# Polysketch attention followed by a squared-ReLU FFN: the sketch features of k in four column tiles of the array, and S loaded repeated over the partitions

## The chip, the cores and the metric

The kernel runs on one core of a Trainium2 chip. The metric is device time in microseconds (us) of one execution; 187.35 us is the median of three runs before the change. A profile of one execution is at hand, with the start and duration of every instruction.

The engines are named as the profile names them: PE is the matrix engine (PEld its weight loads), DVE the vector engine, ACT the scalar engine, POOL the GpSimd engine, SP the engine that issues most of the DMAs.

## The reference, cut to what matters

```python
q, k, v: (4, 4, 1088, 32)   # batch, heads, tokens, head_dim; float32
S1, S2:  (8, 32)
def phi(x):                                   # 64 features per token
    a = einsum('rd,bhsd->bhsr', S1, x)
    b = einsum('rd,bhsd->bhsr', S2, x)
    return einsum('bhsi,bhsj->bhsij', a, b).reshape(..., 64)
q_p, k_p = phi(q), phi(k)
kv  = einsum('bhsf,bhsd->bhfd', k_p, v)       # 64 x 32 per head
z   = k_p.sum(over tokens)
att = (q_p @ kv) / (q_p . z + 1e-6)
x   = att as (4352 tokens, 128)
out = relu(x @ w_in)**2 @ w_out               # w_in (128, 2048), w_out (2048, 128)
```

## The kernel before, in words

**Two stages.** A prologue of some 14 us, written out by hand, computes the sums kv and z of batch 0 and the first 256 columns of xT, the transposed attention output. After it comes the long part: the FFN goes over the 4352 token columns in ten chunks (256, 384, 448, ... wide), each in units of one or two blocks of 128 hidden channels: first matmul (line 589, tile pg), relu on ACT (line 598), square on ACT or DVE (lines 606 and 608), second matmul (line 627, tile po). The attention of the remaining columns and of batches 1 to 3 is woven in between. The order of this part comes from a planner (class `_Order`), which works with fixed costs per operation and due times; the order of each engine's instructions is thus settled when the kernel is built. The diff doesn't touch the planner's entries.

**The prologue, in the order of PE's queue.** (1) Ten matmuls on constants (`keep_warm(W0)`, line 678). (2) `a_kf` (line 311): for the nine 128-token tiles of k, one matmul each (line 314) with the 128 transposed token columns as weights (`kt0`, 128 x 128) and `sf` (128 x 64) as the moving operand. `sf` holds S1 and S2 transposed, once for each of four heads in that head's 32 rows, and zero elsewhere. A float32 matmul appears in the profile as two weight loads and two matmuls, so there are 18 records of each. (3) `q0` (line 729): the sketch of the first 256 query columns, with `sq` as the weights. (4) `a_kv0` (line 390): 36 matmuls that sum the key features times v (tile kvp). (5) The denominator (lines 754 and 794), the products with z (line 801, with `s2f` and `zm`), the spreading of kv (line 433, with `irep`), the numerator (line 794), one warm matmul, the sketch `qc` of the next query columns (line 304), one more warm matmul, and then the FFN's first unit.

**The other engines in the prologue.** DVE transposes k (line 291, tile kt) and S (line 688, tile s_T); it multiplies the key features (`a_kp0`, line 330, four instructions); transposes q (line 297); it makes `bd` and `zm` from kvp (lines 764 and 775), copies kvp (line 773, tile kvt), and makes the reciprocal of the denominator and the first 256 columns of xT (lines 814 to 819). ACT copies half of each kf tile to SBUF (line 320, tile kb). POOL writes constants, copies S into several layouts (lines 693 to 716), converts the four quarters of w_in (line 671) as they land, and fills `sfk` (lines 786 and 789), the weights for the k sketch of later batches.

**S before.** S1 and S2 are loaded once each into 8 rows of a 32 x 32 tile `s_nat` (lines 217 and 218, on ACT's queue, after DVE's memset of line 216). DVE transposes it to `s_T` (32 x 32). From there the layouts are made by copies: four into `sf` (line 693, one per head, on POOL, DVE and ACT), five into `sq` (lines 696 to 703), four more into `sf[:, 64:96]` (line 708), from which `sw` is copied (line 716), and `s2f` is transposed by DVE (line 747).

**Loads.** SP issues, in this order, k (two pieces), q (256 columns), v, the rest of v, q, w_in and w_out. Eight completion counters are used in rotation, and a load waits at issue for the load eight before it to have landed.

## Time and profile before

| what | value |
|---|---|
| median of three runs (187.19 to 187.91) | 187.35 us |
| span of the profiled execution | 186.17 us |
| median less that span, taken as what lies around it (the profiled execution has no time of its own besides the span) | 1.18 us |
| PE busy | 180.4 us, 97% of the span |
| ACT busy | 147.1 us, 79% |
| DVE busy | 108.6 us, 58% |
| POOL busy | 36.5 us, 20% |
| first FFN matmul (line 589) in the timeline | 14.04 us |
| PE busy between 20 and 180 us | 160.00 us of 160.00 |

A line of the timeline gives the start in us, the busy time in us, the engine, the line of the kernel, the operation, the tile written and the tiles read, the shapes, and in brackets the idle time before it and what ended it. Times of single instructions are taken from the records behind that view. The view of one line of the kernel gives minimum, median and maximum of their duration in ns. A line of the chain that ended last gives start, length, and what worked.

### The profile page before, as it was taken

To read this page: it belongs to the slowest core of one execution; us is meant where nothing else is said; L and a number is where in the kernel's file an instruction comes from. 1 tells how busy PE (TensorE), PEld (TensorE's weight loads), DVE (VectorE), ACT (ScalarE), POOL (GpSimd) and SP (SyncE) were. 2 spreads that over 40 slices of the span, in tenths; PEclk is the share of its full clock that TensorE was granted. 3 is DMA by queue.
4 is the path that set the end of the run, shared out by engine and by line. 5 is a ranking of instruction groups with operands and counts; after the bars stand their busy time and mean duration, and the time that the engine had idled before them with its cause. 6 is when DMAs were issued, how large, how long until landed. Compare 5 with 4: busy or idle time off the path is not lost.

```text
span 186.2 us, 3768 instructions
## 1 busy us (share of the span) xinstructions
PE 180.4 (97%) x1417; PEld 105.2 (56%) x1418; DVE 108.6 (58%) x242; ACT 147.1 (79%) x281; POOL 36.5 (20%) x162
## 2 busy tenths in 40 slices
PE   8998999999999999999999999999999999999991
PEld 2766766656555566454554545554545554555791
DVE  4979979969982599599324972997122113112210
ACT  3518769868978887797899897897999999988960
POOL 2745405328300000860000003820000000000000
PEclk9999999999999999999999999999999999999999
DMA  5799800100049500001871200002103000300211
GB/s 185 192 297 310 192 4 5 28 4 0 0 55 267 130 2 4 4 0 24 200 186 19 42 0 4 0 0 38 22 0 58 0 0 0 56 0 0 32 28 28
DMA packets 24673, 11.25 MB, mean 60 GB/s; under 512 B 18000, under 2 KB 23120, under 8 KB 24656
## 3 DMA queue, kind: packets, MB, share of 16 engines
q1 hardware_dynamic: 24144, 10.82, 25.0%
q10 hardware_dynamic: 512, 0.20, 0.4%
q8 instruction: 11, 0.18, 0.4%
q14 instruction: 6, 0.05, 0.1%
HBM read 8.78 MB, written 2.23 MB: 59 GB/s over the span
## 4 chain that ended last, share of the span: by engine, by line
PE 90%; DMA 4%; SPq 1%; POOL 1%; issue 1%; DVE 0%; ACT 0%; ACTq 0%
PE po L627 60%; PE pg L589 18%; PE nd L542 3%; DMA w_in<-in_moe_w_in_dram 3%; PE kvp L408 2%; PE pol L622 2%; PE po L622 2%; PE qc L304 2%; DMA s_nat<-in_S_dram 2%; PE kc L344 1%; SPq L194 1%; POOL sfk L789 0%; ACT gt L598 0%; POOL w_in L671 0%; SPq L203 0%
## 5 line engine op out<-in xcount | busy, mean ns | idle before, releaser
L627 PE MATMUL po<-g,w_o 128*128 128x512 f32 (+3 forms) x288 | 133.0, 546 | 0.3 <-PE pg L589 0.3
L589 PE MATMUL pg<-xT,w_in 128*128 128x512 f32 (+3 forms) x160 | 104.8, 665 | 0.6 <-ACT gt L598 0.5
L598 ACT ACTIVATE gt<-pg 128x512 f32<-128x512 f32 (+3 forms) x145 | 80.7, 561 | 21.7 <-PE pg L589 21.2
L606 ACT ACTIVATE g<-gt 128x512 f32<-128x512 f32 (+2 forms) x122 | 71.8, 603 | 2.7
L627 PEld LDWEIGHTS po<-g,w_o 128*128 128x128 f32 x288 | 53.0, 189 | 30.0 <-issue 19.8
L589 PEld LDWEIGHTS pg<-xT,w_in 128*128 128x128 f32 x160 | 30.1, 189 | 31.7 <-issue 14.3
L608 DVE TENSOR_TENSOR g<-gt 128x512 f32<-128x512 f32 (+3 forms) x23 | 15.1, 660 | 45.9 <-ACT gt L598 45.9
L449 POOL COPY kv<-kvt 32x64 f32<-32x64 f32 x48 | 11.7, 243 | 65.4 <-DVE kvt L426 63.3
L503 POOL COPY rd<-rc 32x9 f32<-32x9 f32 (+2 forms) x80 | 16.7, 209 | 13.1 <-DVE rc L495 9.8
L512 DVE STREAM_SHUFFLE qa<-qc 128x576 f32<-128x576 f32 (+2 forms) x20 | 11.6, 652 | 0.0
L527 DVE TENSOR_TENSOR qp<-qa,qb 128x576 f32<-128x576 f32 (+2 forms) x20 | 10.8, 603 | 0.0
L475 DVE STREAM_TRANSPOSE qt<-qc 128x576 f32<-128x576 f32 (+2 forms) x10 | 5.8, 615 | 5.8 <-PE qc L304 5.8
L631 DVE STREAM_TRANSPOSE oT<-po 128x512 f32<-128x512 f32 (+3 forms) x9 | 5.9, 655 | 5.0 <-PE po L627 5.0
L361 DVE TENSOR_TENSOR kp<-fs 128x576 f32<-128x576 f32 x12 | 8.4, 752 | 0.1
L542 PE MATMUL nd<-qp,kv 32*32 32x288 f32 (+2 forms) x320 | 6.8, 353 | 0.0
L559 DVE TENSOR_TENSOR xT<-nd,bc 128x576 fp32r<-128x576 f32 (+2 forms) x10 | 5.6, 600 | 0.9 <-PE nd L542 0.7
L512 DVE STREAM_SHUFFLE qb<-qc 128x576 f32<-128x576 f32 (+2 forms) x10 | 6.0, 648 | 0.0
L542 PEld LDWEIGHTS nd<-qp,kv 32*32 32x32 f32 x320 | 3.8, 103 | 3.8 <-issue 2.2
L297 DVE STREAM_TRANSPOSE qT<-qn 128x192 f32<-128x192 f32 (+3 forms) x11 | 5.9, 566 | 0.0
L552 DVE STREAM_TRANSPOSE bc<-rd 128x576 f32<-128x576 f32 (+2 forms) x10 | 5.8, 602 | 0.2
L622 PE MATMUL pol<-w_o,g 128*128 128x128 f32 x32 | 5.7, 275 | 0.0
L622 PE MATMUL po<-w_o,g 128*128 128x128 f32 x32 | 5.7, 274 | 0.0
(96 smaller groups left out, 92.3 us busy)
## 6 DMA issues: line engine op xcount, KB each, us to landing
kn<-in_k_dram SPq DMA_DIRECT2D x3, 544.0 KB, 5.4
qn<-in_q_dram SPq DMA_DIRECT2D x3, 544.0 KB, 6.9
vn<-in_v_dram SPq DMA_DIRECT2D x9, 144.0 KB, 5.5
w_in<-in_moe_w_in_dram SPq DMA_DIRECT2D x4, 256.0 KB, 5.2
w_o<-in_moe_w_out_dram SPq DMA_DIRECT2D x4, 256.0 KB, 7.1
out_dram<-oT SPq DMA_DIRECT2D x12, 64.0 KB, 2.0
out_dram<-oT SPq DMA_DIRECT2D x8, 56.0 KB, 1.9
out_dram<-oT SPq DMA_DIRECT2D x8, 48.0 KB, 1.8
```

What stands on the lines that cost most here:

```text
L361: nc.vector.tensor_tensor(out=_ap(st[b, "kp"], 0, 128, 64 * NT * h, [[64, NT], [8, 8], [1, 8]]), in0=_ap(fs, 0, 128, o, [[32, NT], [1, 8], ...
L449: nc.gpsimd.tensor_copy(_ap(st[b, "kv"], 32 * c, 32, 64 * h, [[32, E], [1, 32]]), _ap(st["kvt"], 32 * h, 32, 0, [[64, E], [1, 32]]),)
L503: nc.gpsimd.tensor_copy(st[b, "rd", i0][32 * h : 32 * h + 32, n * c : n * c + n], st["rc"][32 * c : 32 * c + 32, n * h : n * h + n],)
L512: nc.vector.stream_shuffle(in_=banks(st[b, "qc", i0], 2 * x, 0, m), out=_ap(st[b, which, i0], 0, 128, 2 * m * x, [[m, 2], [1, m]]), mask=m ...
L527: nc.vector.tensor_tensor(out=st[b, "qp", i0, e][:, r], in0=st[b, f"qa{e}", i0][:, r], in1=st[b, "qb", i0][:, r], op=mult,)
L542: nc.tensor.matmul(nd[32 * h : 32 * h + 32, 512 * c : 512 * c + m], kv[r, o : o + 32], qp[r, m * h : m * h + m], start=(e == 0), stop=(e = ...
L589: nc.tensor.matmul(st["pg", u][:, n * i : n * i + n], w_in[:, 128 * (d0 + i) : 128 * (d0 + i) + 128], xT[:, c0 : c0 + n],)
L598: nc.scalar.activation(gt[:, 0:w], st["pg", u][:, 0:w], Relu)
L606: nc.scalar.activation(g2[:, 0:w], gt[:, 0:w], Square)
L608: nc.vector.tensor_tensor(out=g2[:, 0:w], in0=gt[:, 0:w], in1=gt[:, 0:w], op=mult)
L622: nc.tensor.matmul(po[x // 128][:, 0:128], g[:, x : x + 128], w, start=(d == 0), stop=(d == NB - 1),)
L627: nc.tensor.matmul(po[0][:, 0:n], w, g, start=(d == 0), stop=(d == NB - 1))
```

## The change

S1 and S2 are each loaded by one DMA that repeats their 8 rows 16 times over the 128 partitions (128 runs of 128 bytes), into the two halves of `s_nat` (128 x 64). S1 is the first DMA of ACT's queue, and S2 is put on SP between the two pieces of k. No memset stands ahead of them. One DVE transpose (128 x 64) then gives S transposed in all partitions.

The copies become products with masks: `own_h` (which 32 rows a partition is in) and `own_q` (even or odd block of 32), made by DVE from the identity matrix. `sf` is one product on POOL; `sq` is two ACT copies with a per-partition scale and one product on POOL; `sw` is a small memset and a copy each; `sfk` is one product on POOL, ahead of the w_in conversions instead of behind them. `s2f` is gone: `s_nat[:, 32:64]` takes its place.

`a_kf` issues four matmuls per 128-token tile, each with 32 columns of weights, into 32 partitions of the output. There are nine warm matmuls in place of ten. Two memsets go from DVE to POOL, the copy of kvp goes from DVE to ACT, `bd`'s second half is made before `zm`, and two transposes of q (`a_qT` at 8 and 14) move from ahead of the `bd` products to behind `zm`.

```diff
-    W0, W3, W4 = 10, 1, 1
+    W0, W3, W4 = 9, 1, 1
...
-    nc.vector.memset(s_nat[:], 0.0)
-    nc.scalar.dma_start(s_nat[0:8, :], S1[:, :])
-    nc.scalar.dma_start(s_nat[8:16, :], S2[:, :])
+    def load_s(eng, x, src):
+        eng.dma_start(
+            s_nat[:, 32 * x : 32 * x + 32],
+            bass.AP(src.tensor, src.offset, [[0, 16], [D, 8], [1, D]]),
+        )
+
+    load_s(nc.scalar, 0, S1)
     load_k(nc.sync, 0, 0, 512)
+    load_s(nc.sync, 1, S2)
     load_k(nc.sync, 0, 512, S)
...
+    nc.vector.tensor_reduce(
+        out=own_h[:, :], in_=_ap(iden, 0, 128, 0, [[32, 4], [1, 32]]), op=add, axis=AX
+    )
+    nc.vector.tensor_tensor(out=own_q[:, :], in0=own_h[:, 0:2], in1=own_h[:, 2:4], op=add)
...
-    nc.vector.memset(kT[:, S:SP], 0.0)
-    nc.vector.memset(qT[:, S:SP], 0.0)
...
-            nc.tensor.matmul(
-                _ap(kf, 0, 128, 32 * t, [[32 * n, 2], [1, 32]]),
-                kt0[:, 128 * (t0 + t) : 128 * (t0 + t) + 128],
-                sf[:, 0:64],
-            )
+            for c in range(4):
+                o = 128 * (t0 + t) + 32 * c
+                nc.tensor.matmul(
+                    _ap(kf, 32 * c, 32, 32 * t, [[32 * n, 2], [1, 32]]),
+                    kt0[:, o : o + 32],
+                    sf[:, :],
+                )
...
+    nc.gpsimd.tensor_tensor(
+        out=_ap(sf, 0, 128, 0, [[32, 2], [8, 4], [1, 8]]),
+        in0=_ap(s_T, 0, 128, 0, [[32, 2], [8, 4], [1, 8]]),
+        in1=_ap(own_h, 0, 128, 0, [[0, 2], [1, 4], [0, 8]]),
+        op=mult,
     )
+    for x in range(2):
+        nc.scalar.activation(
+            _ap(sq, 0, 128, 64 * x, [[8, 8], [1, 8]]), _ap(s_T, 0, 128, 32, [[0, 8], [1, 8]]),
+            Copy, scale=own_q[:, x : x + 1],
+        )
+    nc.gpsimd.tensor_tensor(
+        out=_ap(sq, 0, 128, 128, [[64, 2], [8, 8], [1, 8]]),
+        in0=_ap(s_T, 0, 128, 0, [[0, 2], [1, 8], [0, 8]]),
+        in1=_ap(own_q, 0, 128, 0, [[1, 2], [0, 8], [0, 8]]),
+        op=mult,
     )
...
     for w in sw:
-        nc.gpsimd.tensor_copy(w[:, :], sf[:, 64:96])
+        nc.gpsimd.memset(w[:, 16:32], 0.0)
+        nc.gpsimd.tensor_copy(
+            _ap(w, 0, 128, 0, [[8, 2], [1, 8]]), _ap(s_T, 0, 128, 0, [[32, 2], [1, 8]])
+        )
+    nc.gpsimd.tensor_tensor(
+        out=_ap(sfk, 0, 128, 0, [[16, 2], [8, 2], [1, 8]]),
+        in0=_ap(s_T, 0, 128, 0, [[0, 2], [32, 2], [1, 8]]),
+        in1=_ap(own_q, 0, 128, 0, [[1, 2], [0, 2], [0, 8]]),
+        op=mult,
+    )
+    nc.gpsimd.memset(kT[:, S:SP], 0.0)
+    nc.gpsimd.memset(qT[:, S:SP], 0.0)
...
-    for i0 in (8, 14):
-        a_qT(0, i0, 6)
...
-    nc.vector.tensor_copy(st["kvt"][:, :], st[0, "kvp"][:, 0:128])
-
+    nc.scalar.copy(st["kvt"][:, :], st[0, "kvp"][:, 0:128])
+
+    a_bd(0)
...
-    a_bd(0)
+    for i0 in (8, 14):
+        a_qT(0, i0, 6)
...
-            x0[32 * h : 32 * h + 32, 384:392], s2f[:, :], zm[:, 8 * h : 8 * h + 8],
+            x0[32 * h : 32 * h + 32, 384:392], s_nat[:, 32:64], zm[:, 8 * h : 8 * h + 8],
```

More of the change, by code (lines that the diff above doesn't have):

```diff
@@ L167 @@
     w_in32, w_o, w_in = sb("w_in32", 2048), sb("w_o", 2048), sb("w_in", 2048, F32R)
-    s_nat, s_T = sb("s_nat", 32, rows=32), sb("s_T", 32, rows=32)
+    s_nat, s_T = sb("s_nat", 64), sb("s_T", 64)
     sw = [sb(f"sw{i}", 32) for i in range(2)]
@@ L240 @@
     load_wo(nc.sync, 3)
-    sf, sq = sb("sf", 96), sb("sq", 256)
-    nc.vector.memset(sf[:, 0:64], 0.0)
-    nc.gpsimd.memset(sq[:], 0.0)
+    sf, sq = sb("sf", 64), sb("sq", 256)
     nc.gpsimd.memset(_ap(vn[0], 96, 32, 32 * (NT - 2), [[32 * NT, H], [1, 64]]), 0.0)
@@ L262 @@
     make_identity(nc, iden[:])
-    own_f, s2f, zm = sb("own_f", 16), sb("s2f", 32), sb("zm", 32)
+    own_f, zm = sb("own_f", 16), sb("zm", 32)
+    own_h, own_q = sb("own_h", 4), sb("own_q", 2)
+    nc.vector.tensor_reduce(
+        out=own_h[:, :], in_=_ap(iden, 0, 128, 0, [[32, 4], [1, 32]]), op=add, axis=AX
+    )
+    nc.vector.tensor_tensor(out=own_q[:, :], in0=own_h[:, 0:2], in1=own_h[:, 2:4], op=add)
     nc.vector.tensor_reduce(
@@ L463, in a_w @@
             in0=_ap(st[b, "kvp"], 0, 128, 32, [[64, E], [8, 4], [1, 8]]),
-            in1=_ap(sf, 0, 128, 72, [[0, E], [0, 4], [1, 8]]),
+            in1=_ap(s_T, 0, 128, 32, [[0, E], [0, 4], [1, 8]]),
             op=mult,
@@ L688 @@
     nc.vector.transpose(s_T[:, :], s_nat[:, :])
-    for h, eng in (
-        (0, nc.gpsimd.tensor_copy), (1, nc.vector.tensor_copy), (2, nc.scalar.copy),
-        (3, nc.vector.tensor_copy),
-    ):
-        eng(
-            _ap(sf, 32 * h, 32, 8 * h, [[32, 2], [1, 8]]), _ap(s_T, 0, 32, 0, [[8, 2], [1, 8]])
-        )
-    nc.gpsimd.tensor_copy(
-        _ap(sq, 0, 32, 0, [[8, 8], [1, 8]]), _ap(s_T, 0, 32, 8, [[0, 8], [1, 8]])
-    )
-    nc.scalar.copy(
-        _ap(sq, 0, 32, 128, [[8, 8], [1, 8]]), _ap(s_T, 0, 32, 0, [[1, 8], [0, 8]])
-    )
-    for h, eng in ((1, nc.scalar.copy), (2, nc.gpsimd.tensor_copy), (3, nc.scalar.copy)):
-        eng(
-            _ap(sq, 32 * h, 32, 64 * (h % 2), [[128, 2], [1, 64]]),
-            _ap(sq, 0, 32, 0, [[128, 2], [1, 64]]),
-        )
-    for h in range(H):
-        nc.gpsimd.tensor_copy(sf[32 * h : 32 * h + 32, 64:96], s_T[:, :])
+    nc.gpsimd.tensor_tensor(
[8 more added lines that the diff above has]
+            Copy, scale=own_q[:, x : x + 1],
+        )
+    nc.gpsimd.tensor_tensor(
[3 more added lines that the diff above has]
+        op=mult,
+    )
     for h in range(H):
@@ L745 @@
             a_kv0(t)
-    nc.vector.transpose(s2f[:, :], _ap(sf, 0, 128, 72, [[0, 4], [1, 8]]))
     nc.vector.tensor_tensor(
@@ L785 @@
         cast_wi(c)
-    nc.gpsimd.memset(sfk[:], 0.0)
-    for h in range(H):
-        o = 16 * (h % 2)
-        nc.gpsimd.tensor_copy(sfk[32 * h : 32 * h + 32, o : o + 16], s_T[:, 0:16])
     num0 = psf.tile([128, 512], F32, tag="pg", name="num0")
```

## The prediction

> **What bounds the kernel now.** I read the waits of PE first. From 14 us to the end only two kinds of pause are listed:

> ```profile
> PE pg L589 <- ACT gt L598: 0.5, 1, 0.5
> PE po L627 <- PE pg L589: 0.3, 1, 0.3
> ```

> Apart from these 0.8 us, all at the start of the FFN, PE works without a pause from its first FFN matmul (14.04 us) to the end. The change leaves this work alone, so what it is worth is how much earlier the FFN starts. Next I read the timeline of the prologue:

> ```profile
> 0.77 4.42 PE L678 MATMUL warm<-const-bfloat16-1.0 128*128 128x512 bf16 x10 [0.77 <-PEq L1078]
> ...
> 4.48 0.20 DVE L688 STREAM_TRANSPOSE s_T<-s_nat 32x32 f32<-32x32 f32 x1 [0.28 <-DMA s_nat<-in_S_dram]
> 4.72 0.42 DVE L693 COPY sf<-s_T 32x16 f32<-32x16 f32 x2
> ```

> ```profile
> 7.61 1.13 PE L729 MATMUL x<-qT,sq 64*128 64x256 f32 x8
> ...
> 8.68 2.32 PE L390 MATMUL kvp<-vn,kp 128*64 128x64 f32 x72
> ...
> 13.47 0.42 DVE L819 TENSOR_TENSOR xT<-num,bc 128x256 fp32r<-128x256 f32 x1
> ```

> S lands at 4.38 (last landing record), is transposed to 4.68, copied into `sf` to 5.14, and PE's kf begins at 5.26. From there PE goes from one group to the next: kf 5.26 to 7.46, q0 7.61, kvp 8.67, then the chain of small products up to `qc` (13.60) and the warm matmul after it (13.98 to 14.19). Each change of tile shape costs about 0.09 (end of streaming to next load: 8.58 to 8.67, 10.82 to 10.92, 13.89 to 13.98). The first FFN matmul follows at 14.2. xT, which it needs, is done at 13.90, so the path is PE's own chain, with 0.3 us of room on DVE. The chain of waits names POOL's `sfk` ahead of `qc`, but that is chance: `qc` starts 0.09 after the warm matmul's 0.21 us of streaming, as after every change of shape.

> The lines of kf:

> ```profile
> L314 PEld LDWEIGHTS kf<-sf,kt x18: 192/192/333, 5.3 to 7.3; 128*128 128x128 f32 x18
> L314 PE MATMUL kf<-sf,kt x18: 275/275/444, 5.3 to 7.4; 128*128 128x64 f32 x18
> ```

> The maxima are the first records. Up to 5.7 us they are up to 0.214 apart, after that 0.112. The warm matmuls, too, come every 0.427, while 512 columns take 0.213 later. So PE runs at half speed until about 5.7 us, although the clock column says 1.00 throughout.

> **The change, part by part.**

> *S lands earlier.* Before, S1 waits for a memset (issue 0.92 to 1.49), S2 follows on the same queue (1.52 to 1.81) and lands 2.57 after that issue. After, S1 needs no memset and can go at about 0.74, as the first k load does; S2 goes second on SP, where a load is issued every 0.47: end of issue 1.62. S is 256 runs of 128 bytes; a run of that size took 13 ns in the trace, so 16 runs per DMA engine are 0.2 us. Between the first k piece (landed 3.47) and the second (4.28) that gives S at 3.6 to 3.9. In DVE's queue the transpose of S stands behind that of the first k piece (3.49, 0.71 long, the next can start 0.08 before its end), so it starts at 4.15. For 64 columns I take 0.20 (32 columns) + 32 x 1.0 ns (the slope between 336 ns for 192 and 402 ns for 256) = 0.24: done at 4.40.

> *`sf` by one product on POOL.* No POOL product is in the trace. POOL copies take 0.21 (128x32) and 0.62 (128x512, a conversion), thus 0.24 for 64 columns; a second operand could double it: 0.24 to 0.50. I take 0.30, nearer to the copies, whose fixed part is most of it. With 0.06 from DVE to POOL, as before, `sf` is ready at 4.76 and kf starts at 4.83: **0.43 earlier**. The ninth warm matmul ends at 4.57 (0.77 + 9 x 0.427), so PE still waits 0.26, as it did (4.99 to 5.26).

> [...]

> *kf in four column tiles.* The shape is in the trace, in the later batches (line 408: 128 x 32 weights, 64 columns moving, four column tiles). From the chain that ended last:

> ```profile
> 38.28 1.25 PE kvp L408 x80
> ```

> 80 records in 1.25 us are 15.6 ns each; inside the group a round of four comes every 0.056. kf becomes 72 records, 18 rounds: 18 x 0.056 = 1.0 us at full speed, against 18 x 0.112 = 2.0. At half speed I take 0.107 a round (0.427 for 512 columns, and a float32 record streams its 64 columns twice). From 4.83 to 5.7 run 8.2 rounds, the other 9.8 take 0.55: streaming ends at 6.26 instead of 7.46. With 0.12 for the change of shape (0.15 before) q0 starts at 6.38 instead of 7.61: **1.23 earlier** in all. A later `sf` costs only half of its delay while half speed lasts. The transposed k is there: with one more issue ahead the second k piece lands at 4.6, its transposes end at 5.15 and 5.45, and rounds 9 and 15 need them at 5.7 and 6.0.

> [...]

> *What must keep up.* q's transpose waits for q, which lands at 5.3 (5.01 before, one issue later), and ends at 5.75; q0 needs it at 6.38. The key products on DVE start behind it, at 5.85 (6.40 before), and take 2.75: end 8.6. kvp then runs 7.45 to 9.6 and needs the last of them for its tiles 7 and 8, at 9.1. `sq` is done by 5.2 (two ACT copies of 0.24, one POOL product of 0.3 to 0.5). So kvp and all after it move by 1.23. If DVE were late here, kvp would wait with it, at most 0.2.

> *Moved work.* The two q transposes (0.63 of DVE issue) now stand between `zm` and the denominator's transpose. That one starts 1.16 after the first `bd` product because it waits for PE; the DVE work in between is 0.21 + 0.20 + 0.10 + 0.63 = 1.14. It fits, and xT has 0.3 of room behind it. kvt's copy (0.28) goes to ACT, idle there for 3.6 us. `s2f` (0.20) was on idle DVE time. POOL's 0.86 for `sfk` and the five `sf` and `sw` copies (1.2) were covered by POOL's idle time behind PE's chain; nothing waited for them. The new POOL products, memsets and copies end by 8.6, before the w_in conversions (9.9), which wait for DMA. If that cover went, the conversions would start later by as much.

> *Start of the FFN.* Two stalls there are read here:

> ```profile
> 14.57 1.20 POOL L671 CAST w_in<-w_in 128x512 fp32r<-128x512 f32 x2 [1.00 <-DMA w_in<-in_moe_w_in_dram]
> ...
> 15.22 1.16 DVE L608 TENSOR_TENSOR g<-gt 128x256 f32<-128x256 f32 x2
> ```

> The first square took 0.83 while POOL converted w_in; the second 0.41. PE waited for it until 16.14. The conversions are tied to the landings (14.45, 15.09) and don't move. The first square, 1.23 earlier, runs at 14.0 to 14.4 before them: up to 0.44 more. Against that stand what still waits for DMA and POOL: unit 5 needs the third quarter of w_in (ready 15.18) and now asks at about 15.5; the 16 POOL copies of line 503 can't start before the conversions end (15.77, 16.88 before), so the next columns of xT, ready at 22.06 and used at 22.52, move by 1.1 + 0.46 at most. So between 0 and 0.35 more; I take **0.2**.

> **Sum:** 0.43 + 0.80 (kf) + 0.2 = 1.43 us. Span 186.17 - 1.43 = 184.74; with the 1.18 around it, 185.92. The median shown is that same 187.35.

> **The rivals.** (A) As worked out: 185.9, its own range 185.3 to 186.5. (B) *The gain is partly given back to DMA and POOL.* The engines' share was 1.04 to 1.10 between 10.9 and 20 us, so S2's extra 0.47 on SP may pass to the last w_in quarters. SP had waits for landings between 3.0 and 4.7, which speaks against it. Then line 503 starts at 16.3, the next xT moves by 0.58 + 0.46 = 1.04: 186.3; with unit 5 also held, 186.6. (C) *The column tiles do not overlap*, and a record costs the 31 ns of line 390's two tiles (2.25 / 72): kf takes 2.2 and only the 0.43 is left: 186.9. Line 408 speaks against. (D) *Slower: half speed lasts longer.* Nine warm matmuls, a pause and smaller tiles may not open the clock at 5.7. Every us of half speed beyond costs 0.5, so the 1.23 is gone if it lasts to 8.2. Until the end of q0: kf ends at 6.76, q0 takes 2.1 and ends at 9.0, where kvp started at 8.67: 187.7; through kvp as well, 189.3. For it: the pause comes earlier than before. Against: it has the same length, and ten matmuls at half speed sufficed.

> [...] The trace shows one opening, 4.9 us after the first matmul.

> **How the numbers follow.** A 0.66, B 0.17, C 0.10, D 0.07. Low end: clock open before kf (0.2 more) and the whole 0.35 at the FFN, with S product at 0.24: 185.1. High end: `sf` no earlier than before (4 rounds at half speed, then 14: q0 at 6.6, 1.0 gained), less 0.5 given back, 186.85; to take in C, 187.1. Within 0.5% (0.94 us, about what a measurement of this kernel tells from no change) are C, the upper part of B, and most of D. Faster by more: A with 0.64 and part of B, 0.11; slower by more: the long form of D.

> **What would show it.** kf at 4.8 with 72 records in 1.4 us, rounds 0.056 apart from 5.7 on; q0 at 6.4; kvp at 7.5; first FFN matmul near 13.0; first square 0.4 long. Wrong would be: S landing after 4.2, the POOL product over 0.6, kf rounds of 0.12 at full speed, half speed beyond 6 us, kvp waiting for DVE, or PE pauses between 14 and 22 us larger than 0.8.

## The result and the profile after

The changed kernel is **slower**, by 1.0%: 189.44 us (median of 11 runs, 188.12 to 190.78) against 187.35 us (11 runs, 187.18 to 188.01), a ratio of 1.0104 with an interval of 1.0081 to 1.0128. The forecast was 185.9, at most 187.1. The profiled execution of the changed kernel took 188.31 us, the second shortest of the eleven, with a span of 186.5 us. Ratios in this document leave out runs that the comparison counts as disturbed (before has some at 190.8 to 191.2, e3 four of ten, e16 four of twelve, e2 two of ten, e8 to e12 one each), while medians take all runs, and the profiles of e8 and e9 are of such runs.

The waits of PE after the change, to be set against the two that the prediction showed (columns: total, times, longest, in us):

```profile
PE kf L322 <- DVE kt L297: 1.4, 1, 1.4
PE kf L322 <- POOL sf L697: 0.7, 1, 0.7
PE pg L597 <- ACT gt L606: 0.5, 1, 0.5
PE po L635 <- PE pg L597: 0.2, 1, 0.2
```

The two pauses at the start of the FFN are as they were. New are 2.1 us of pause in kf: ahead of it for `sf`, and in its middle for the transposed k. The timeline of the prologue shows who was late:

```profile
0.74 0.64 ACTq L217 DMA_DIRECT2D s_nat<-in_S_dram  x1
...
1.19 0.66 SPq L217 DMA_DIRECT2D s_nat<-in_S_dram  x1
...
1.48 1.09 ACTq L194 DMA_DIRECT2D vn<-in_v_dram  x2
...
1.90 0.57 SPq L176 DMA_DIRECT2D kn<-in_k_dram  x1
...
4.75 0.25 DVE L696 STREAM_TRANSPOSE s_T<-s_nat 128x64 f32<-128x64 f32 x1 [0.57 <-DMA s_nat<-in_S_dram]
...
5.08 0.29 POOL L697 TENSOR_TENSOR sf<-s_T,own_h 128x64 f32<-128x64 f32 x1 [3.35 <-DVE s_T L696]
...
5.43 0.65 PE L322 MATMUL kf<-sf,kt 128*32 128x64 f32 x32 [0.66 <-POOL sf L697]
...
6.86 0.84 DVE L297 STREAM_TRANSPOSE kt<-kn 128x384 f32<-128x384 f32 x2 [1.86 <-DMA kn<-in_k_dram]
...
7.49 0.78 PE L322 MATMUL kf<-sf,kt 128*32 128x64 f32 x40 [1.41 <-DVE kt L297]
```

Read it from below: kf's second half begins at 7.49 because DVE could transpose the second piece of k only at 6.86, and DVE waited 1.86 us for its DMA. That load was issued at 1.90 (1.19 before), behind S2's issue, which took 0.66 us. Beside it ACT issued two loads of v, at 1.48 and 2.05; before, the second of them waited until 3.49 for the completion counter of k's first piece, which landed at 3.47. The landing records: the 16 parts of k's second piece land from 4.85 to 6.84 (3.87 to 4.28 before), S2's from 3.45 to 4.65.

So q0 starts at 8.20 (forecast 6.38, before 7.61), and the first FFN matmul at 14.91 (before 14.04, in a second profile of before 13.77, forecast 13.0). Before the change, and after it:

```profile
14.04 0.80 PE L589 MATMUL pg<-xT,w_in 128*128 128x256 f32 x4
```

```profile
14.91 0.71 PE L597 MATMUL pg<-xT,w_in 128*128 128x256 f32 x4
```

Two of the pieces are as forecast: the product on POOL took 0.29 us, and the rounds of kf follow each other by 0.056 us.

### The profile page after: what moved, and what is told of

The parts are those of the page before. It is cut to its first block, busy times and chain, and to the rows that moved or that the text cites. A ratio compares the mean times of both kernels' runs of the same rounds, so it can differ in the third digit from the quotient of the medians.

```text
span 186.5 us, 3858 instructions
## 1 busy us (share of the span) xinstructions
PE 179.4 (96%) x1471; PEld 103.8 (56%) x1471; DVE 108.0 (58%) x236; ACT 146.8 (79%) x280; POOL 35.0 (19%) x156
## 4 chain that ended last, share of the span: by engine, by line
PE 94%; DMA 3%; SPq 1%; DVE 0%; ACT 0%; issue 0%
PE po L635 60%; PE pg L597 18%; PE nd L550 3%; DMA kn<-in_k_dram 3%; PE kvp L416 2%; PE pol L630 2%; PE po L630 2%; PE qc L310 2%; PE kvp L398 1%; PE kc L352 1%; PE x L745 1%; PE kf L322 0%; ACT gt L606 0%; SPq L217 0%; PE warm L686 0%
## 5 line engine op out<-in xcount | busy, mean ns | idle before, releaser
L616 DVE TENSOR_TENSOR g<-gt 128x512 f32<-128x512 f32 (+3 forms) x23 | 15.5, 677 | 45.9 <-ACT gt L606 45.9
```

Of the source, the lines that this page charges most:

```text
L616: nc.vector.tensor_tensor(out=g2[:, 0:w], in0=gt[:, 0:w], in1=gt[:, 0:w], op=mult)
```

## The experiments

Theories, as their forecasts name them. **T1**: S2's place and its long issue on SP delay k's second piece, PE pauses, and its clock closes. **T2**: the 256 runs of 128 bytes disturb the queues wherever they are issued. **T3**: column tiles or fewer warm matmuls keep the clock down themselves. **T4**: a pause of PE does. **T5**: v's two early loads on ACT hold k back. **T6** came late: PE's own program arrives too late. All ratios are to the kernel before on the same chip.

### The changed kernel again

**e1**: no edit.

> The changed kernel once more, unaltered, for a second profile: its runs spread from 188.1 to 190.8 us with mean clocks from 0.991 to 1.000. Theory T1 (the second piece of k lands late because S2 stands ahead of it on SP; PE pauses about 1.5 us in the middle of kf; in most executions the clock gate then closes for a few us): again 189 to 190, PE waiting 1 to 2 us for DVE's transpose of k inside kf, and where the mean clock is 0.991 a stretch of matmuls at half speed after the pause. Theory T3 (the column tiles or the smaller number of warm matmuls keep the clock down by themselves): half speed from the first kf record on, before any pause.

189.22 us (4 runs), ratio 1.0117 [1.0083, 1.0150]. k's second piece lands at 4.71 to 6.19, kf waits 0.8 us for it (T1 gave 1 to 2). The slowdown and the late piece repeat. PE also stands 0.6 us in the group `kc`, which comes up again below.

### One part at a time

**e2, kf in column tiles alone** (and e12, the same kernel again): the kernel before with this edit.

```diff
+            for c in range(4):
+                o = 128 * (t0 + t) + 32 * c
-                _ap(kf, 0, 128, 32 * t, [[32 * n, 2], [1, 32]]),
-                kt0[:, 128 * (t0 + t) : 128 * (t0 + t) + 128],
+                    _ap(kf, 32 * c, 32, 32 * t, [[32 * n, 2], [1, 32]]),
+                    kt0[:, o : o + 32],
```

> Before, with kf alone in four column tiles; S, loads and ten warm matmuls as before. T1: kf's rounds take 0.056 us at full speed, nothing waits for k, 186.3 to 186.7 us (0.7 to 1.0 faster than before). T3 (tiles or clock): 187.3 or slower.

187.88 us (10 runs, 186.30 to 190.07), ratio 1.0006 [0.9980, 1.0032]: no gain at the median, so T1's 186.3 to 186.7 is missed. Yet the profiled execution is the 186.30, and its timeline shows the forecast gain:

```profile
5.12 1.30 PE L316 MATMUL kf<-sf,kt 128*32 128x64 f32 x72 [0.16 <-ACT sq L701]
6.35 1.19 PE L731 MATMUL x<-qT,sq 64*128 64x256 f32 x8
```

1.30 us instead of 2.2 (e5 below), q0 at 6.35, the first FFN matmul at 12.84, 0.93 before the 13.77 of the second profile of before. The column tiles do overlap. Most of its other executions don't keep this gain; why is found below.

72 records in 1.30 us are 18 ns each, loads included: near the 15.6 of line 408, far from the 31 of rival C. The clock is open from 4.58 us in this profile, so all of kf runs at full speed.

**e3, the loads alone**: the kernel before with the repeated loads of S, its copies reading the new layout.

> Before, with only the loads of S as in the change (repeated over 128 partitions, S1 first on ACT, S2 on SP between the two pieces of k) and the copies of S reading the new layout; kf in 128-column tiles. T1: the second piece of k lands at 5.5 to 7 us and kf waits for it: 188.5 to 190.5. T3: the loads are harmless: 187.0 to 187.5.

189.32 us (10 runs), ratio 1.0063 [1.0030, 1.0096]. k's second piece lands at 4.31 to 6.50, and full-width kf waits 0.6 us for it:

```profile
PE kf L319 <- DVE kt L296: 0.6, 1, 0.6
```

The loads alone make the kernel slower, by the ratios some six tenths of what the whole change loses; that they are harmless (T3) is ruled out.

**e5, before again**: 187.31 us (1 run), span 185.5.

> Before, unaltered, for a second profile: 19 runs of it beside the last experiments lay at 186.8 to 187.7 with two at 190.8. All theories: 186.8 to 187.7, first FFN matmul 0.3 to 1.0 earlier than in the first profile (which belongs to one of its slower runs), the clock open before kf.

kf at 5.22, q0 at 7.34, first FFN matmul at 13.77. The profile that the prediction was made from has a span of 186.17, 0.6 longer: it was one of the longer executions of this kernel.

### Which of the loads

**e4**: the changed kernel with k's second piece ahead of S2 on SP.

```diff
-    load_s(nc.sync, 1, S2)
     load_k(nc.sync, 0, 512, S)
+    load_s(nc.sync, 1, S2)
```

> The change with S2's load moved on SP behind the second piece of k, nothing else. T1: k's second piece lands near 4.3 to 4.6, kf starts at about 5.3 and doesn't pause: 186.2 to 186.9. Rival T2 (it is not the place on SP, but the traffic itself: the 256 short runs of S, or v's loads on ACT's queue that now go out earlier, disturb k's second piece): it lands at 5.5 or later still, 188 to 189.5.

189.44 us (4 runs), ratio 1.0114 [1.0072, 1.0155]. k now lands by 4.83, but S2 by 5.38, so the pause only changes its place. Neither forecast holds: not T1's 186.2 to 186.9, nor T2's landing of k at 5.5 or later. Its timeline, and the granted clock by stretch (columns: stretch, its length, PE busy and matmuls, clock, DMA share, GB/s):

```profile
6.16 1.56 PE L322 MATMUL kf<-sf,kt 128*32 128x64 f32 x72 [1.97 <-POOL sf L697]
7.65 2.08 PE L745 MATMUL x<-qT,sq 64*128 64x256 f32 x8
```

```profile
5.00:7.00 2.00, 0.84 (x56) 0.97 0.76 173
7.00:9.00 2.00, 2.00 (x34) 0.50 0.93 209
9.00:11.00 2.00, 2.00 (x40) 0.68 0.66 192
```

After a pause of 2.0 us the clock, open since 3.45, falls to half from 6.86 to 10.28, 3.41 us by the clock's record: q0 takes 2.08 us for 1.13. Such a stretch makes the mean clock of an execution 0.991. In the changed kernel 5 of 11 executions have a mean of 0.991, in e1 2 of 4; in 116 runs of before, none.

**e6**: both loads of S on ACT.

```diff
+    load_s(nc.scalar, 1, S2)
     load_k(nc.sync, 0, 0, 512)
-    load_s(nc.sync, 1, S2)
```

> The change with both loads of S on ACT's queue; SP starts with the two pieces of k as before. Theory T1 (S2's place and its 0.66 us of issue on SP hold k back): k's second piece lands at 4.3 to 4.8, S at 4.0 to 4.6, kf starts by 5.2 and doesn't pause: 186.3 to 187.3. Rival T2 (the 256 short runs disturb k's load wherever they are issued): it lands at 5.5 or later, 188 to 189.5.

188.57 us (10 runs), ratio 1.0050 [1.0025, 1.0075]. k's second piece lands at 3.94 to 4.36, as before the change; S2 lands by 5.40, kf starts at 6.18. By the ratio half of the loss goes; the time is above T1's 186.3 to 187.3, and T2's late k did not come. In this profile the clock opens only at 9.14, so kf takes 2.15 us.

**e8**: the kernel before with S2's eight narrow runs on SP between the pieces of k.

```diff
-    nc.scalar.dma_start(s_nat[8:16, :], S2[:, :])
     load_k(nc.sync, 0, 0, 512)
+    nc.sync.dma_start(s_nat[8:16, :], S2[:, :])
```

> Before, with S2's load (8 runs, as before) put on SP between the two pieces of k. If the place on SP is what holds k back (T1), k's second piece lands at 5 us or later and it is 188 to 189.5. If it is the 128 short runs and their 0.66 us of issue (T2), k lands at 4.5 to 4.8 and it is 187.0 to 187.8.

187.44 us (10 runs), ratio 0.9991 [0.9973, 1.0009]. The place on SP by itself costs the median nothing, and neither do early loads of v: ACT issues them here at 1.60 and 2.00, as in the changed kernel. It takes the wide loads as well. The only profile is of the longest of the ten executions (191.00 us), and in it k's second piece is late without a wide load, landing at 4.00 to 6.15:

```profile
PE kf L314 <- DVE kt L291: 1.0, 1, 1.0
```

So the late piece can come without them, but the median doesn't show it.

**e9, v's two early loads moved to SP** in the changed kernel; e10, the same in e2's kernel.

```diff
-    load_v(nc.scalar, 0, 2, 0, 4)
+    load_v(nc.sync, 0, 2, 0, 4)
-    load_v(nc.scalar, 0, 3, 0, 4)
+    load_v(nc.sync, 0, 3, 0, 4)
```

> The change with the two early loads of v that ACT issues (at 1.48 and 2.05 us there; before, the second one waited until 3.49) moved to SP, behind the first pieces of k and q. Theory T5 (these 256 runs of 512 bytes on ACT's queue go out beside k's second piece and hold it back, together with S's 0.66 us of issue): k's second piece lands at 4.5 to 5.2 with its 16 parts within 0.6 us, kf hardly pauses: 186.5 to 187.8. Rival T2 (S's 128-byte runs alone upset the queues): it lands at 5.5 or later with a spread over 1 us: 188.5 to 189.5.

> Before with kf in column tiles (as in the run of kf alone) and the two loads of v moved from ACT to SP. If kf alone varied (186.3 to 190.1) because its faster kf waits for late landings of k and q: landings earlier and closer together, median 186.2 to 187.0, spread under 1.2 us. If it varied for the clock gate alone: as kf alone, 187.5 to 188.

e9: 188.43 us (11 runs), ratio 1.0042 [1.0007, 1.0077], 1.0 less than the changed kernel. S2 now lands at 3.31 to 3.75, inside the forecast 3.6 to 3.9, kf starts at 4.70, k's second piece lands at 4.44 to 5.53 and costs 0.4 us of wait in place of 1.4:

```profile
PE kf L322 <- DVE kt L297: 0.4, 1, 0.4
```

This profile is of the longest of the eleven executions (191.65 us); in e15 and e17 below, with the same loads, k's second piece lands by 5.39 and 5.52, and S2 by 4.59 and 3.90. So T5 holds for half of the loss: with the same loads of S, only v's loads moved. Its 186.5 to 187.8 is missed. e10: 187.69 us (10 runs), ratio 1.0017 [0.9986, 1.0047]: without S's repeated loads there is nothing to gain from it, and the 186.2 to 187.0 of earlier landings is missed.

### Filling the pause

**e7 and e11**: four more warm matmuls behind kf's second tile group, written into tile pg (e7) or x0 (e11).

```diff
+    st["warm"] = x0
+    keep_warm(4)
```

> The change with four more warm matmuls between the second and the third group of kf, in the pause where PE waits for k. Theory T4 (the pause lets the clock gate close again for 3.4 us in about half of the executions): mean clocks of 0.99 and below are gone and the runs draw together at 187.5 to 188.6. Rival (the closing comes from the small products later): clocks and spread stay, 189 to 190.

> The change with four warm matmuls in the pause inside kf, now written into the tile x0, so that no later part of kf waits for their buffer (the 1.2 us wait of the earlier try). Theory T4 (the pause lets the clock gate close): no mean clock at or below 0.991, 187.8 to 188.9, spread under 1.2 us. Rival: as the change, 189 to 190 with a third of the clocks at 0.991.

189.65 us, ratio 1.0124 [1.0083, 1.0166], and 191.08 us, ratio 1.0175 [1.0067, 1.0282]. e7's clock stays open in all four executions, as T4 wants, but kf's last group then waits 1.2 us for its buffer. e11 has 1.65 us of pause at `kc`, 26 us into the run, 1.0 for xT, and one execution of four with a mean clock of 0.988. Both are above T4's ranges, and neither tells how much the clock is worth.

### Where the column tiles' gain goes

**e12**, e2's kernel again:

> kf alone in column tiles once more, on the same chip as the version with v on SP, and for the profile of another execution. Median 187.3 to 188.2 as before; where the profiled run is above 187, PE waits inside or just behind kf for the transposes of k or q, or works at half speed beyond 6 us.

187.66 us (10 runs), ratio 1.0022 [1.0004, 1.0041]. In its profile the FFN starts at 13.06, 0.7 before e5, and the span is 186.0, 0.4 longer. The wait that takes the gain back is not inside or just behind kf, as forecast, but in the middle of the FFN's first part, in `kc`, the sketch of the next batch's k. In e12 and, larger, in e9:

```profile
22.68 0.71 PE L346 MATMUL kc<-kT,sfk 64*32 64x288 f32 x14
24.24 0.67 PE L346 MATMUL kc<-kT,sfk 64*32 64x288 f32 x2 [0.85 <-issue]
```

```profile
23.51 0.71 PE L352 MATMUL kc<-kT,sfk 64*32 64x288 f32 x15
26.74 0.57 PE L352 MATMUL kc<-kT,sfk 64*32 64x288 f32 x1 [2.51 <-issue]
```

PE stops inside a group of like matmuls, for nothing that the profile names ("issue"). It costs more than the pause itself: from `kc`'s first matmul to the 1100th matmul before the end, eleven profiles need 2.90 us, that of before among them, and e12 4.41, e9 7.43. So e12 loses 1.5 us here. The view of the DMA queues gives the hint. For e9, from 13 to 24.3 us and then from 24.3 to 25.5 (columns: packets, MB, share of the engines):

```profile
q1 hardware_dynamic: 2858, 2.98, 95.6%
q14 instruction: 1, 0.01, 0.3%
```

```profile
q8 instruction: 1, 0.02, 5.3%
q1 hardware_dynamic: 6, 0.01, 2.0%
```

An instruction queue (q8) brings eleven packets of 16384 bytes in each run, which I take for program code. In e12 three of them come after 951, 1208 and 1454 of PE's 2943 records (in the changed kernel after 950, 1207 and 1452), so I take these for PE's, with some 256 records in one. This is an estimate: in before the eleven come 136 to 348 records apart. In e9 none comes from 13 to 24.3 us, while loads keep the DMA engines 96% busy; then one, from 24.36 to 25.38, and PE goes on at 26.74. Six profiles have a pause of 0.37 us or more there (e1, e9 to e12, e18). In each PE resumes 1.24 to 1.5 us after the packet's end, and in each it had stopped after nearly the same number of its records, 683 to 685, although that is now the 12th, now the 15th or 16th matmul of `kc`. In these six the place thus goes with the count of records and not with the work. In before, PE starts its 685th record at 29.89, some six us later; a packet is done at 23.64, and whether it is the one that PE needs there is not shown.

The tiles make kf 72 matmul records instead of 18, and as many weight loads: 108 more, the first part of the page counts 1471 matmuls for 1417. By the estimate of 256 that is 0.42 of a packet, and a block of code ends inside `kc`, where without them it ended six us later. If its successor is asked for when the block before begins, 256 records earlier, that moves from 20.2 us (before) to 12.7 (e12), into the time in which w_in, w_out and the next batch's k, v and q are loaded. This is T6. When the block is asked for is an assumption, and loads don't always hold it up: in the profile of the changed kernel, in e2 and in e13 the packet came amid the loads, at 19.06, 15.99 and 17.14, and these three have no pause at `kc`. In e9 the granted clock is at half behind the pause of 2.5 us, from 26.83 to 30.25.

**e13, more code alone**: the kernel before, its ten warm matmuls replaced by 72 small ones.

```diff
-    keep_warm(W0)
+    for _ in range(72):
+        nc.tensor.matmul(
+            st["warm"][0:32, 0:72],
+            nc.const_aps.tensor(1.0, (128, 32), mybir.dt.bfloat16),
+            nc.const_aps.tensor(1.0, (128, 72), mybir.dt.bfloat16),
+        )
```

> The kernel before with its ten warm matmuls replaced by 72 of 72 columns with 32 columns of weights: the same streaming (5184 columns for 5120), 62 instructions pairs more in PE's program (124 records), about as many as the column tiles of kf add (108). Nothing else is changed. T6 (code): PE's program arrives in blocks of 16 KB on the instruction queue; in the kernels with column tiles the second block of the run lands at 23 to 25.4 us, and in five of their profiles PE stands 0.4 to 2.5 us inside the group kc, ended by issue, until 1.24 to 1.40 after that landing. With 124 records more, the block ends inside or just behind kc here too, so the profile shows a pause of PE that is ended by issue at 24 to 27 us in at least half of the executions, 0.3 to 2 long, and the median is 187.8 to 188.6 for 187.4 before. T3 (clock): 32 columns of weights keep the clock down longer, which the clock record shows as an opening after 6 us, with no pause at kc: 187.6 to 189. If neither holds: 187.3 to 187.6.

188.15 us (12 runs, 187.30 to 189.19), ratio 1.0029 [1.0009, 1.0049] (before there: 187.67). kf starts at 5.33 and the clock opens at 5.15, so T3's late clock is not seen. The median is in T6's range. But the profiled execution is the fastest one, 187.30, its code packet came at 17.14, and it has no pause at `kc`: the mechanism isn't seen in this run, and what makes the median longer stays open.

**e14, fewer instructions**: e2's kernel with the first two k tiles full width, 24 records fewer.

```diff
+            if t0 == 0:
+                nc.tensor.matmul(
+                    _ap(kf, 0, 128, 32 * t, [[32 * n, 2], [1, 32]]),
+                    kt0[:, 128 * (t0 + t) : 128 * (t0 + t) + 128],
+                    sf[:, 0:64],
+                )
+                continue
             for c in range(4):
```

> The kernel before with column tiles in seven of the nine k tiles; the first two, which run while half speed lasts, stay full width. That is 24 records fewer in PE's program than with all nine, and 0.1 to 0.2 us more of kf. T6: the end of the code block moves 24 records back, from inside kc to some ten FFN pairs of 0.3 us behind it, about 3 us later, so the block is there in time: no pause at kc, first FFN matmul at 12.9 to 13.3, median 186.3 to 186.8, where kf_only and its repeat gave 187.9 and 187.7. T1, T3 and T5 (loads or clock alone make the column tiles' gain vanish): 187.6 to 188.0 as before, and no difference at kc.

187.06 us (12 runs, 186.52 to 187.68), ratio **0.9964 [0.9951, 0.9976]**: the only version faster than before, 0.3 above the range that T6 gave. The intervals of e2 and e12, with all nine tiles, lie above this one. Its code packet is as late as the others (21.93 to 23.25), but PE starts its 685th record only at 26.48, and `kc` runs through:

```profile
23.73 0.72 PE L353 MATMUL kc<-kT,sfk 64*32 64x288 f32 x16
24.38 1.13 PE L636 MATMUL po<-g,w_o 128*128 128x256 f32 x4
```

This profile is the slowest of its twelve: kf starts at 5.33, and at the FFN's start PE waits for a conversion that is tied to a landing, as the prediction feared:

```profile
PE kf L315 <- ACT sq L708: 0.9, 1, 0.9
PE pg L598 <- POOL w_in L680: 0.7, 1, 0.7
```

**e15 and e16**: the same edit in e9's kernel and in the changed kernel.

> The changed kernel with v's two later loads on SP, as in e9, and the first two k tiles full width. e9's profile has its first FFN matmul at 13.82 and then 2.5 us of pause in kc, ended by issue. T6: that pause goes in nearly all executions: median 187.3 to 187.9 for 188.4 there. If the pause comes from something else: 188.3 to 188.6.

> The changed kernel with the first two k tiles full width and nothing else. The late second k piece and the clock's second stretch of half speed stay (T1, T4, T5), the pause at kc (0.0 and 0.6 in the two profiles of the changed kernel) goes: 188.7 to 189.3 for 189.3. If T6 is the larger part of the changed kernel's loss, under 188.5; if it has no part, 189.2 to 189.6.

e15: 187.48 us (12 runs), ratio 1.0013 [0.9987, 1.0040], in T6's range and 1.0 below e9, and its profile has no pause at `kc`; but the ratio's interval overlaps that of e9, so the gain is not clear of the noise. e16: 189.31 us (12 runs, 187.76 to 190.94), ratio 1.0055 [1.0030, 1.0079]. Its median is the changed kernel's, its ratio is lower than the 1.0104 there, and whether this edit alone helps the changed kernel stays open. Its profile has no pause at `kc` either, and k's piece late (4.81 to 6.64, 0.8 us of wait in kf).

**e17 and e18**: ten warm matmuls again, in e15's kernel and in the changed kernel.

```diff
-    W0, W3, W4 = 9, 1, 1
+    W0, W3, W4 = 10, 1, 1
```

> e15 (the changed kernel, v's two later loads on SP, the first two k tiles full width) with ten warm matmuls in place of nine. e15's twelve executions fall into two groups, spans of 185.1 to 185.6 and of 186.4 to 187.1; the profiled one, of the second group, has its clock open only at 9.20 us, after a pause of PE from 4.8 to 5.4. T4 (the pause keeps the clock down): the tenth warm matmul fills 0.21 to 0.43 of the 0.6 us, so the second group gets smaller or vanishes: median 187.0 to 187.3 for 187.48, hardly a span above 186. If the pause is not the cause: two groups as before, 187.4 to 187.9.

> The changed kernel with ten warm matmuls in place of nine, nothing else. T4 with the ninth and tenth warm matmul as its cause: fewer executions with a late clock, 188.6 to 189.0 for 189.4. T1 and T5 (the second k piece lands late because of S's second load and v's early loads on ACT): the long pause is inside kf, 1.4 us of it behind the eighth round, and no warm matmul ahead of kf fills it, so nothing changes: 189.1 to 189.6.

e17: 187.42 us (12 runs), ratio 0.9994 [0.9981, 1.0007], just over T4's 187.0 to 187.3 and inside the 187.4 to 187.9 of the rival. The second group of e15 (5 of 12 spans between 186.4 and 187.1) has shrunk to one span of twelve above 186, as T4 wants; twelve executions of each don't settle it. The two profiles, e15 first, show what such a group can be:

```profile
6.41 1.72 PE L329 MATMUL kf<-sf,kt 128*32 128x64 f32 x56
8.06 1.68 PE L752 MATMUL x<-qT,sq 64*128 64x256 f32 x8
```

```profile
5.48 0.43 PE L329 MATMUL kf<-sf,kt 128*32 128x64 f32 x16
6.17 0.78 PE L329 MATMUL kf<-sf,kt 128*32 128x64 f32 x40 [0.26 <-DVE kt L297]
6.89 1.13 PE L752 MATMUL x<-qT,sq 64*128 64x256 f32 x8
```

e15's clock opens at 9.20 us, after a pause of 0.6 us ahead of kf, and kf and q0 run at half speed; with the tenth warm matmul the pause is gone and the clock is open at 4.99. e18: 189.43 us (6 runs), ratio 1.0096 [1.0068, 1.0124], no gain, as T1 and T5 had it: its pause of 1.2 us is inside kf, where no warm matmul stands, and it has 0.9 us of pause at `kc`.

| kernel | median, us | ratio to before |
|---|---|---|
| changed | 189.44 | 1.0104 |
| changed, v on SP (e9) | 188.43 | 1.0042 |
| the same, two k tiles full width (e15) | 187.48 | 1.0013 |
| the same, ten warm matmuls (e17) | 187.42 | 0.9994 |
| before with e14's column tiles | 187.06 | 0.9964 |

## Why the prediction was wrong, point by point

**"With one more issue ahead the second k piece lands at 4.6"** is the step that failed. One issue was priced by SP's usual 0.47 us and the landing moved by 0.3. The issue of 128 runs took 0.66, the load went out 0.71 later, and it landed at 6.84 (e1 6.19), so that PE stood 1.4 us inside kf. About 1 us of this lateness goes with v's two loads, which went out beside it: without them it landed by 5.39 to 5.53 (e9, e15, e17). The change of S's loads had shifted which completion counter those wait for: before, the second went out at 3.49, behind the landing of k's first piece at 3.47, and after it at 2.05 without a wait. The rotation of the counters stood in the text on the kernel before; the prediction didn't follow it. The rest goes with the wide load of S2 ahead of it on SP: with that on ACT, where v's loads go out later too (2.14 and 3.69), it landed by 4.36 (e6). e9's median, 1.0 us lower, shows the share of v's loads in the time, e8's that the place without the wide load costs nothing.

**S at 3.6 to 3.9, kf at 4.83**: 4.65 and 5.43. The price of the runs themselves was about right: with v's loads out of the way S2 lands by 3.75 in e9, though by 4.59 in e15. What was missing is, by e9, the other traffic; e15 leaves a part open.

**kf: 1.0 us less at the same start; q0 at 6.38**: right in kind (0.056 a round), lost in the changed kernel to the 1.4 us of pause. That e2's q0 starts at 6.35 is partly luck: its kf starts 0.29 later than forecast, but the clock was open, where the forecast has half speed until 5.7. That rounds 9 and 15 would have their k was the cover of this edit, and the cover had 0.55 us of room (transposes done at 5.15 and 5.45, needed at 5.7 and 6.0).

**"Apart from these 0.8 us PE works without a pause"** was taken as a property of everything behind 14 us. It holds for before; with 108 more records six profiles have a pause at `kc`, up to 2.5 us long (e9), and that PE's code is late there is T6's reading. No line of the profile of before shows this wait; the number of records and the instruction queue's packets, on which T6 rests, weren't read. In e12 the pause is 0.85 and the loss 1.5, more than the 0.7 gained ahead of the FFN.

**Rival D** ("half speed lasts longer", 0.07, 187.7 to 189.3) came nearest, with its price about right: half of a stretch of 3.41 us is 1.7. That its number is near is in part luck, since the changed kernel's profiled execution has the clock open from 5.20 and loses its time to the late loads. Where half speed does last or come back, it follows pauses of 2.0 us (e4), 1.4 (e6) and 0.6 (e15), behind S landed by 5.38, 5.40 and 4.59; its "same length" of the pause was the assumption that broke. Not each pause is followed by it: after the changed kernel's 1.4 us the clock stayed open. What the tenth warm matmul is worth is not shown: no gain in the changed kernel (e18), and 0.06 us at the median where v's loads are moved (e17). The prediction had one opening to go by, at 5.7; in the runs the clock opened at 3.45 (e4), 5.20 (the changed kernel), 9.14 (e6) and 9.20 (e15), and what sets the moment is not shown.

**kvt's copy "to ACT, idle there"**: ACT was idle, but the copy reads the same tile as the two `bd` products, and the three run one after the other:

```profile
11.63 0.29 DVE L776 TENSOR_TENSOR bd<-kvp,own_p 128x128 f32<-128x128 f32 x1 [0.38 <-PE kvp L398]
...
11.96 0.27 ACT L785 COPY kvt<-kvp 128x128 f32<-128x128 f32 x1 [1.99 <-DVE bd L776]
...
12.26 0.29 DVE L776 TENSOR_TENSOR bd<-kvp,own_p 128x128 f32<-128x128 f32 x1 [0.33 <-ACT kvt L785]
...
13.11 0.41 DVE L824 STREAM_TRANSPOSE dT<-den 128x256 f32<-128x256 f32 x1
```

The second `bd` product so starts 0.3 us late, and what stands behind it no longer fits: the prediction gave 1.14 us from the first `bd` product to the denominator's transpose, and it is 1.48. From the first `bd` product to the first FFN matmul all eleven profiles with this edit need 3.28 us, the nine without it 2.88 to 3.07. In the changed kernel q0 is 0.59 us later than before and the FFN 0.87; the 0.28 between them is this. It wasn't taken out by itself.

**"1.18 around the span"**: 1.8 to 2.1 us in the runs. The span of 186.17 was not that of the median execution; a sum against the median should have been made against a span of 185.5.

**Right**: the product on POOL (0.29 for 0.30), the transpose of S (0.25 for 0.24), POOL's moved work, which nothing waited for.

**What stays open**: each run profiles one execution. How the changed kernel's 2.1 us divide over its executions between the late piece, the clock and the pause at `kc` follows from the steps of e9, e15 and e17, not from profiles of each, and only the step of e9 is clear of the noise; and some of its executions, 190.4 us at a mean clock of 1.0, have no profile that explains them.

## What to carry to other kernels

Before a load is put ahead of another, list every load near it with its queue and the counter it waits for, and ask which ones the change lets go earlier: a late operand came here from loads that the diff doesn't name, going out beside one that it widened. A faster form that issues four times the instructions also brings PE to a given count of records earlier, to the 685th at 24.91 us in the changed kernel and at 29.89 before, and the pauses at `kc` stood behind 683 to 685 records. Count the records, find the instruction queue's packets, and look for one that lands late while the DMA engines are full (96% busy in e9). And when one part shortens a stage, look at what it had covered: two us of full-width matmuls hid that k's second piece, with the loads as before, lands anywhere from 4.2 (e2) to 5.0 us (e13).
